# A fused convolution and two feed-forward layers on one core: the first 64 units as whole products, one a step

## The chip, the cores and the metric

The kernel runs on one core of one Trainium2 chip. The metric is the device time of one execution in microseconds (us); smaller is better. Times of a kernel are medians of several executions, and a profile shows one execution of its own.

## What is computed

The input holds 2 x 4096 tokens of 192 channels, in float32. A causal convolution with 7 taps (softmax weights, eight groups of 24 channels) is followed by two feed-forward layers, 192 to 2048 to 192, the first with a piecewise quadratic activation, the second with an approximate GELU:

```python
out = einsum('hk,bskhg->bshg', softmax(weight), windows(x))     # 7 taps, per head
h = x @ w_in;  g = where(h >= 1, h, where(h <= -1, 0, (h + 1)**2 / 4));  x = g @ w_out
h = x @ w_in2; g = h * sigmoid(1.702 * h);                      y = g @ w_out2
```

## The kernel before, in words

**Tiles and units.** Tokens lie along the free dimension, in 16 blocks of 512. One layer of one block is a *phase* (list `phases`, L211). The 2048 hidden channels are 16 tiles of 128, and a *unit* is one hidden tile of one phase: `gemm1` makes the hidden tile, `act_a` and `act_b` make its activation, and `gemm2` adds its part of the output to the phase's two accumulator banks. There are 512 units. The first 64 belong to four phases, two and two of them taken in turn, four hidden tiles at a time (L215), since the weights are converted while these units run. From unit 64 on a phase's 16 units follow each other.

**Precision.** Each operand is split into a high and a low part (`split`, L72: ScalarE rounds, another engine subtracts), and a product is made of high x high, high x low and low x high. With 128 channels in one tile (`ah`, `al`) and the other 64 in a tile of their high parts over their low parts (`b`), `gemm1` (L233) is five products of 128 rows by 512 columns, and `gemm2` (L297) is five.

**Couples of 64-row products.** `both(u, v)` (L324) runs the products of units u and u+1 of the first layer product and v and v+1 of the second, v = u - 4, as pieces of 64 rows. The lower and the upper half of the array work on different pieces at the same time. One of gemm1's pieces (low x low) is left out, so that two units make 19 pairs of pieces, where whole products would be 20. For this the 64-row pieces need a second tile `c` with the halves of `b` swapped, which `swap_halves` (L178) makes by two transfers on SP's queue. Where one bank goes from one half of the array to the other, TensorE pauses (L350).

**Order of the work.** Everything is issued by one loop (L469) over couples of units, and every engine takes its instructions in that order. An iteration issues `both`, then `act_a` and `act_b` of units u and u+1 (ScalarE: two functions and a rounding; VectorE: one operation; the subtraction on GpSimd for the first 48 units, L280, then on VectorE), then `finish` of a phase that is done, then whatever `plan` holds for the steps u and u+1. The plan (`at`, L387) holds, by step:
- the conversion of each weight tile from 64-bit words, in four pieces in four successive steps (`weight_ops`, L103 to L136): `begin` (ScalarE, two VectorE operations), `join` (VectorE), `high_part` (ScalarE) and `low_part` (GpSimd or VectorE, L133 and L134). Its load is issued three steps earlier. In layer 1, tile f from 8 on begins in step 2f - 9; in layer 2, tile f begins in step 27 + 2f;
- the convolutions of coming blocks, a tap a step on VectorE (L154); for blocks 2 and 3 the first 16 of these operations are in steps 10 to 25. Block 1's main convolution is done by TensorE in steps 0 to 2 (L171);
- the second half of `finish`, one and two steps after its first.

The first four units (two couples) run as whole products, since no second-layer product is there yet; so do the second-layer products of the last four, in the drain.

The edges of the banks: four banks in turn take hidden tiles (unit modulo 4), two and two take accumulators. Three buffers hold activations, four their high and low parts.

Of the kernel before, what the change touches and what calls it, by code (L numbers as in the profile page):

```python
# [20 lines left out]
def kernel(  # L21
# [26 lines left out]
    B = P // DB  # L48
    PAD = K - 1
    H = P // 2  # L50
    LAG = 4
    CH = 4
    EARLY = 3 * NF

    const = ctx.enter_context(tc.tile_pool(name="const", bufs=1))
# [93 lines left out]
    def conv_taps(part, t, c):  # L149
        def tap(k):  # L150
            w, x = taps[:, part, k : k + 1], t[:, k : k + T]
            if k == 0:
                return lambda: nc.vector.tensor_scalar_mul(c, x, w)
            return lambda: nc.vector.scalar_tensor_tensor(c, x, w, c, op0=ALU.mult, op1=ALU.add)  # L154

        return [tap(k) for k in range(K)]
# [21 lines left out]
    def swap_halves(dst, src):  # L178
        nc.sync.dma_start(f32(dst[0:DB]), f32(src[DB:P]))
        nc.sync.dma_start(f32(dst[DB:P]), f32(src[0:DB]))  # L180

    def put_b(i, c, step=0):

        b = i % B
        t, other = x1[i][2 + b], x1[i][3 - b]
        hi, lo = (t[0:DB], t[DB:P]) if b == 0 else (t[DB:P], t[0:DB])
        split(c[b * DB : (b + 1) * DB], hi, lo)
        at(step, lambda: swap_halves(other, t))

    def conv_ops(j):  # L190

        ta, tb = xt[0, B * j], xt[1, j]
        ca = cv_p.tile([P, T], F32, tag="cva", name="cva")
        cb = cv_p.tile([P, T], F32, tag="cvb", name="cvb", bufs=1)
        x1[B * j] = new_xs()
        ops = conv_taps(0, ta, ca) + [lambda: put_a(B * j, ca)]
        ops += conv_taps(1, tb, cb) + [lambda: put_b(B * j, cb, now[0])]
        st = {}

        def begin():  # L200
            st["c"] = cv_p.tile([P, T], F32, tag="cva", name="cva")
            x1[B * j + 1] = new_xs()
            st["ops"] = conv_taps(0, xt[0, B * j + 1], st["c"])
            put_b(B * j + 1, cb, now[0])

        ops.append(begin)
        ops += [lambda: st["ops"].pop(0)() for _ in range(K)] + [lambda: put_a(B * j + 1, st["c"])]
        return ops
# [24 lines left out]
    def gemm1(u):  # L233

        ah, al, b, _ = x_of(u)
        h = hid[u] = bank(HID + u % 4, f"h{u}")
        hi, lo = hidden_w(u)
        prods = [
            (lo[:, 0:P], ah),
            (hi[:, 0:P], al),  # L240
            (hi[:, 0:P], ah),
            (lo[:, P : 2 * P], b),
            (hi[:, P : 2 * P], b),
        ]
        for j, (w, r) in enumerate(prods):
            nc.tensor.matmul(h, w, r, start=j == 0, stop=j == len(prods) - 1)
# [14 lines left out]
    def act_a(u):  # L261

        n, _ = phases[units[u][0]]
        h = hid.pop(u)
        a = a_p.tile([P, T], F32, tag="a", name="a")
        if n == 1:

            nc.scalar.activation(a, h, AF.Relu, bias=0.5, scale=0.5)  # L268
            nc.scalar.activation(a, a, AF.Square)  # L269
            nc.vector.scalar_tensor_tensor(a, h, 1.0, a, op0=ALU.max, op1=ALU.min)  # L270
        else:
            nc.scalar.activation(a, h, AF.Sigmoid, scale=1.702)  # L272
            nc.vector.tensor_mul(a, h, a)  # L273
        act[u] = a

    def act_b(u):
        a = act.pop(u)
        hi = g_p.tile([P, T], F32R, tag="ghi", name="ghi")
        lo = g_p.tile([P, T], F32R, tag="glo", name="glo")
        split(a, hi, lo, nc.gpsimd if u < EARLY else nc.vector)  # L280
        halves[u] = (hi, lo)
# [4 lines left out]
    def acc_tiles(p):  # L286
        accs[p] = [bank(k, f"acc{k}_{p}") for k in acc_banks(p)]
        return accs[p]
# [8 lines left out]
    def gemm2(u):  # L297

        p, f = units[u]
        acc_a, acc_b = accs[p]  # L300
        hi, lo = halves.pop(u)
        wh, wl, wb = out_w(u)
        first, last = units[u][1] == 0, units[u][1] == NF - 1
        nc.tensor.matmul(acc_a, wl, hi, start=first, stop=False)
        nc.tensor.matmul(acc_a, wh, hi, start=False, stop=False)
        nc.tensor.matmul(acc_b, wb, hi, start=first, stop=False)
        nc.tensor.matmul(acc_b, wb, lo, start=False, stop=last)
        nc.tensor.matmul(acc_a, wh, lo, start=False, stop=last)
# [52 lines left out]
    def finish(p, step):  # L361
        n, i = phases[p]
        acc_a, acc_b = accs.pop(p)
        if n == 1:
            ah, al, b, c = x2[i] = new_xs()
            s = cv_p.tile([P, T], F32, tag="cva", name="s")
            nc.scalar.copy(s[0:DB], acc_b[DB:P])
            split(acc_a, ah, al)
            at(step + 1, lambda: nc.vector.tensor_add(s[0:DB], acc_b[0:DB], s[0:DB]))

            def put():
                split(s[0:DB], b[0:DB], b[DB:P])
                swap_halves(c, b)

            at(step + 2, put)
        else:
            o = o_p.tile([P, 2, T], F32, tag="o", name="o")
            nc.scalar.copy(o[0:DB, 1], acc_b[DB:P])
            nc.scalar.copy(o[:, 0], acc_a)
            nc.vector.tensor_add(o[0:DB, 1], acc_b[0:DB], o[0:DB, 1])  # L380
            nc.sync.dma_start(out[i, 0:P], o[:, 0])
            nc.sync.dma_start(out[i, P:D], o[0:DB, 1])


    plan, xt, raw, now = {}, {}, {}, [0]

    def at(step, op):  # L387
        plan.setdefault(max(step, 0), []).append(op)
# [28 lines left out]
    with tc.manual_schedule():  # L417
        nc.sync.dma_start(taps, taps_in)
        fetch_x((0, 0), (1, 0))
        fetch_w(1, 0)  # L420
        fetch_w(1, 1)
        fetch_x((0, 1))
        fetch_w(1, 2)

        make_identity(nc, ident)
        warm_up()
        softmax_taps()

        nc.scalar.activation(const.tile([P, 1], F32, name="table"), ident[:, 0:1], AF.Sigmoid)
        for i in range(B):  # L430
            x1[i] = new_xs()
        ca = cv_p.tile([P, T], F32, tag="cva", name="cva")
        cb_ps, ca_ps = bank(3, "cb_ps"), bank(2, "ca_ps")
        a0 = conv_taps(0, xt[0, 0], ca)
        b_ops = conv_on_pe(1, xt[1, 0], cb_ps, ident, nc.scalar.mul)
        a1 = conv_on_pe(0, xt[0, 1], ca_ps, ident, nc.gpsimd.tensor_scalar_mul)
        for op in b_ops:
            op()

        ws = [weight_ops(1, f, raw.pop((1, f)), nc.gpsimd if f else nc.vector) for f in range(CH - 1)]  # L440
        order = a0[0:3] + ws[0][0:1] + a0[3:5] + ws[0][1:3] + a0[5:7] + ws[0][3:4] + ws[1][0:1]
        order += [lambda: put_a(0, ca)] + ws[1][1:2] + [lambda: put_b(0, cb_ps)] + ws[1][2:] + ws[2]
        for op in order:
            op()
        fetch_w(1, 3)
        for k, op in enumerate(weights_at(1, 3, nc.gpsimd)):
            at(k // 2, op)
        for k, op in enumerate(a1):
            at((k + 2) // 3, op)
        at(1, lambda: put_b(1, cb_ps, 1))  # L450
        at(2, lambda: put_a(1, ca_ps))

        def convert_at(n, f, steps):
            eng = nc.vector if (n, f) < (1, 2 * CH) or n == 2 and f % 2 else nc.gpsimd
            at(steps[0] - 3, lambda: fetch_w(n, f))
            for step, op in zip(steps, weights_at(n, f, eng)):
                at(step, op)

        for f in range(CH, NF):
            s = f - 2 if f < 2 * CH else 2 * f - 2 * CH - 1  # L460
            convert_at(1, f, range(s, s + 4))
        for f in range(NF):
            s = 2 * NF - 5 + 2 * f
            convert_at(2, f, range(s, s + 4))
        for j in range(1, NBLK // B):
            conv_at(j)


        for u in range(0, len(units) + LAG + 4, 2):  # L469
            v = u - LAG  # L470
            if u < len(units) and v >= 0:
                both(u, v)
            elif u < len(units):
                gemm1(u)
                gemm1(u + 1)
            elif v < len(units):
                gemm2(v)
                gemm2(v + 1)
            if u < len(units):
                for op in (act_a, act_b):  # L480
                    op(u)
                    op(u + 1)
            if 0 <= v < len(units) and units[v + 1][1] == NF - 1:
                finish(units[v][0], u + 1)
            for step in (u, u + 1):
                now[0] = step
                for op in plan.get(step, []):
                    op()


# [53 lines left out]
```

## Time and profile before

| what | before |
|---|---|
| median of 3 runs | 1246.87 us (1246.42 to 1248.4) |
| the profiled execution, own time | 1247.26 us |
| span of its trace | 1245.5 us |
| TensorE busy (matmul) | 1186.8 us, 95% |
| VectorE busy | 910.8 us, 73% |
| ScalarE busy | 847.8 us, 68% |
| GpSimd busy | 105.4 us, 8%, all of it in the first 230 us |
| mean granted clock of TensorE | 0.971 |

The span is the time between the first and the last instruction; the profiled execution's own time is 1.8 us more. Busy time of TensorE counts pipelined matmuls, and a matmul of 64 rows shows as one record per half of the array. The granted clock is a share of 2.4 GHz; it stands at 1.0 or at 0.5 (1.2 GHz), and a number between them is a mean over a stretch. In the trace PE is TensorE and PEld its weight loads, DVE VectorE, ACT ScalarE, POOL GpSimd, and SP the queue that issues transfers.

### The profile page before, as it was taken

How to read it: one execution, taken by the hardware profiler on the slowest of the kernel's cores; microseconds unless marked ns; L12 is line 12 of the kernel's file. 1: busy time of each engine (PE TensorE's matmuls, PEld its weight loads, DVE VectorE, ACT ScalarE, POOL GpSimd, SP SyncE). 2: the span in 40 equal slices, each digit the busy share in tenths (PEclk: the TensorE clock that was granted, in tenths of full speed). 3: DMA queues.
4: the chain of work that ended last, by engine and by line, in shares of the span. 5: the costliest groups of instructions: out<-in, count | busy, mean ns of one | idle time of the engine just before them, and what ended most of it. 6: DMA issues, size and time to landing. Idle time of an engine off the chain costs nothing.

```text
span 1245.5 us, 24069 instructions
## 1 busy us (share of the span) xinstructions
PE 1186.8 (95%) x9738; PEld 969.2 (78%) x9738; DVE 910.8 (73%) x1354; ACT 847.8 (68%) x1467; POOL 105.4 (8%) x99
## 2 busy tenths in 40 slices
PE   7777878899999999999999999999999999999998
PEld 4555557688888888888888888888888888888886
DVE  6786787686967678686967778686876778686665
ACT  5555765668676776867677676867677686867754
POOL 4366453000000000000000000000000000000000
PEclk8878888899999999999999999999999999999999
DMA  4321122011000000001000010001000010000000
GB/s 146 103 72 39 52 87 72 1 31 39 10 22 10 26 23 18 14 18 40 10 22 9 10 40 18 14 18 40 7 25 10 10 39 19 14 18 14 1 19 18
DMA packets 17023, 37.28 MB, mean 30 GB/s; under 512 B 2576, under 2 KB 2576, under 8 KB 16912
## 3 DMA queue, kind: packets, MB, share of 16 engines
q1 hardware_dynamic: 16912, 35.74, 9.7%
q8 instruction: 77, 1.26, 0.4%
q14 instruction: 34, 0.28, 0.1%
HBM read 21.05 MB, written 6.29 MB: 22 GB/s over the span
## 4 chain that ended last, share of the span: by engine, by line
PE 85%; DVE 6%; ACT 3%; POOL 3%; issue 2%; DMA 0%; SPq 0%; POOLq 0%; DVEq 0%; ACTq 0%
PE acc L353 44%; PE h L353 40%; POOL glo L74 2%; DVE wd L124 1%; DVE wd L117 1%; ACT a L268 1%; ACT a L269 1%; DVE a L270 1%; POOL wt L133 1%; DVE wt L133 1%; DVE cva L154 1%; ACT ghi L73 1%; DVE wd L118 0%; DMA raw<-in_w_dram 0%; PE ca_ps L171 0%
## 5 line engine op out<-in xcount | busy, mean ns | idle before, releaser
L353 PE MATMUL acc<-ghi,wt 64*128 64x512 f32 x3048 | 1009.7, 397 | 0.7 <-ACT ghi L73 0.7
L353 PE MATMUL h<-xah,wt 64*128 64x512 f32 x2032 | 808.6, 398 | 39.9 <-POOL wt L133 20.2
L353 PE MATMUL acc<-glo,wt 64*128 64x512 f32 x2032 | 808.6, 398 | 2.7 <-POOL glo L74 2.6
L353 PEld LDWEIGHTS acc<-ghi,wt 64*128 64x128 f32 x3048 | 569.5, 187 | 63.9 <-ACT ghi L73 2.0
L353 PEld LDWEIGHTS h<-xah,wt 64*128 64x128 f32 x2032 | 380.6, 187 | 88.0 <-POOL wt L133 23.7
L353 PEld LDWEIGHTS acc<-glo,wt 64*128 64x128 f32 x2032 | 380.7, 187 | 46.0 <-POOL glo L74 4.3
L353 PE MATMUL h<-xal,wt 64*128 64x512 f32 x1016 | 403.8, 397 | 0.2 <-DVE xal L74 0.2
L73 ACT CAST ghi<-a 128x512 fp32r<-128x512 f32 x512 | 313.7, 616 | 107.7 <-DVE a L273 63.6
L74 DVE TENSOR_TENSOR glo<-a,ghi 128x512 fp32r<-128x512 f32 x464 | 313.2, 687 | 20.2
L270 DVE SCALAR_TENSOR_TENSOR a<-h,a 128x512 f32<-128x512 f32 x256 | 176.2, 690 | 196.8 <-ACT a L269 196.2
L353 PE MATMUL h<-xb,wt 64*128 64x512 f32 x762 | 261.5, 396 | 3.3 <-ACT xb L73 3.3
L353 PE MATMUL h<-xc,wt 64*128 64x512 f32 x762 | 260.7, 395 | 0.4 <-DMA xc<-xb 0.4
L273 DVE TENSOR_TENSOR a<-h,a 128x512 f32<-128x512 f32 x256 | 169.9, 687 | 78.6 <-ACT a L272 77.9
L272 ACT ACTIVATE a<-h 128x512 f32<-128x512 f32 x256 | 149.4, 596 | 105.7 <-PE h L353 64.1
L353 PEld LDWEIGHTS h<-xal,wt 64*128 64x128 f32 x1016 | 190.7, 188 | 19.9 <-DVE xal L74 0.5
L268 ACT ACTIVATE a<-h 128x512 f32<-128x512 f32 x256 | 152.5, 596 | 78.6 <-PE h L353 65.6
L269 ACT ACTIVATE a<-a 128x512 f32<-128x512 f32 x256 | 161.9, 632 | 8.2
L353 PEld LDWEIGHTS h<-xc,wt 64*128 64x128 f32 x762 | 142.1, 186 | 20.8 <-DMA xc<-xb 1.1
L353 PEld LDWEIGHTS h<-xb,wt 64*128 64x128 f32 x762 | 141.4, 186 | 14.0 <-ACT xb L73 3.6
L74 POOL TENSOR_TENSOR glo<-a,ghi 128x512 fp32r<-128x512 f32 x48 | 69.6, 1469 | 84.0 <-ACT ghi L73 71.1
L154 DVE SCALAR_TENSOR_TENSOR cva<-xt,taps,cva 128x512 f32<-128x512 f32 x90 | 70.5, 784 | 1.3
L129 ACT CAST wt<-wd 128x448 fp32r<-128x448 f32 x32 | 18.1, 566 | 41.1 <-DVE wd L124 41.1
(72 smaller groups left out, 403.7 us busy)
## 6 DMA issues: line engine op xcount, KB each, us to landing
raw<-in_w_dram SPq DMA_DIRECT2D x32, 448.0 KB, 3.4
xc<-xb SPq DMA_DIRECT2D x48, 128.0 KB, 2.2
xt<-in_xa_dram SPq DMA_DIRECT2D x16, 259.0 KB, 3.3
out_dram<-o SPq DMA_DIRECT2D x16, 256.0 KB, 2.0
xt<-in_xb_dram SPq DMA_DIRECT2D x8, 259.0 KB, 3.1
xb<-xc SPq DMA_DIRECT2D x16, 128.0 KB, 2.2
out_dram<-o SPq DMA_DIRECT2D x16, 128.0 KB, 2.3
taps<-in_taps_dram SPq DMA_DIRECT2D x1, 7.0 KB, 1.6
```

The source lines that it names most:

```text
L73: nc.scalar.copy(hi, src)
L74: (eng or nc.vector).tensor_sub(lo, src, f32(hi))
L117: nc.vector.tensor_single_scalar(d, low, 29, op=ALU.logical_shift_right)
L129: nc.scalar.copy(w[:, 0:WC], f32(st["d"]))
L133: eng.tensor_sub(w[:, WC + DB : 2 * WC], d[:, 0:m], f32(w[:, 0:m]))
L154: return lambda: nc.vector.scalar_tensor_tensor(c, x, w, c, op0=ALU.mult, op1=ALU.add)
L268: nc.scalar.activation(a, h, AF.Relu, bias=0.5, scale=0.5)
L269: nc.scalar.activation(a, a, AF.Square)
L270: nc.vector.scalar_tensor_tensor(a, h, 1.0, a, op0=ALU.max, op1=ALU.min)
L272: nc.scalar.activation(a, h, AF.Sigmoid, scale=1.702)
L273: nc.vector.tensor_mul(a, h, a)
L353: mm = nc.tensor.matmul(banks[n], w, r, start=n in fresh, stop=ends.get(n) == k)
```

## The change

The first 64 units (`WHOLE`) no longer run in couples of 64-row pieces. A step handles one unit: `gemm1(step)` as five whole products, `act_a(step)`, `act_b(step - 1)`, `gemm2(step - 3)` as five whole products, `finish` of a phase whose last unit is four behind, and the plan's entries of the step. Unit 64's iteration is a transition: `gemm1(64)`, `gemm2(61)`, `gemm1(65)`; from unit 66 on `both` runs as before. The copies with swapped halves are made only for phases whose units start at 64 or later, and at once where before they were entered into the plan of the same step.

```diff
+    WHOLE = 4 * NF
-    def put_b(i, c, step=0):
-        b = i % B
-        t, other = x1[i][2 + b], x1[i][3 - b]
+    def put_b(i, c):
+        b, halved = i % B, phases.index((1, i)) * NF >= WHOLE
+        t = x1[i][2 + (b if halved else 0)]
         hi, lo = (t[0:DB], t[DB:P]) if b == 0 else (t[DB:P], t[0:DB])
         split(c[b * DB : (b + 1) * DB], hi, lo)
-        at(step, lambda: swap_halves(other, t))
+        if halved:
+            swap_halves(x1[i][3 - b], t)
...
     def gemm2(u):
         p, f = units[u]
+        if f == 0:
+            acc_tiles(p)
...
                 split(s[0:DB], b[0:DB], b[DB:P])
-                swap_halves(c, b)
+                if phases.index((2, i)) * NF >= WHOLE:
+                    swap_halves(c, b)
...
+        def beside(step):
+            for op in plan.get(step, []):
+                op()
+
+        def finish_if_last(u, step):
+            if 0 <= u < len(units) and units[u][1] == NF - 1:
+                finish(units[u][0], step)
+
+        for step in range(WHOLE):
+            gemm1(step)
+            act_a(step)
+            if step >= 1:
+                act_b(step - 1)
+            if step >= LAG - 1:
+                gemm2(step - LAG + 1)
+            finish_if_last(step - LAG, step)
+            beside(step)
+
+        act_b(WHOLE - 1)
-        for u in range(0, len(units) + LAG + 4, 2):
+        for u in range(WHOLE, len(units) + LAG + 4, 2):
             v = u - LAG
-            if u < len(units) and v >= 0:
+            if u == WHOLE:
+                gemm1(u)
+                gemm2(v + 1)
+                gemm1(u + 1)
+            elif u < len(units):
                 both(u, v)
-            elif u < len(units):
-                gemm1(u)
-                gemm1(u + 1)
             elif v < len(units):
                 gemm2(v)
                 gemm2(v + 1)
...
-            if 0 <= v < len(units) and units[v + 1][1] == NF - 1:
-                finish(units[v][0], u + 1)
+            finish_if_last(v + 1, u + 1)
             for step in (u, u + 1):
-                now[0] = step
-                for op in plan.get(step, []):
-                    op()
+                beside(step)
```

## Rows read from the trace of the kernel before

**Rows 1.** The page: span, and TensorE, VectorE and granted clock in 40 slices.

```profile
span 1245.5 us, 24069 instructions
...
PE   7777878899999999999999999999999999999998
...
DVE  6786787686967678686967778686876778686665
...
PEclk8878888899999999999999999999999999999999
```

**Rows 2.** Table of stretches, cut at starts of couples 4, 10, 26, 48, 66.

```profile
core 0: us, PE busy (x) PEld busy (x) DVE busy (x) ACT busy (x) POOL busy (x), PEclk, DMA share, GB/s
0.00:34.18 34.18, 26.72 (x67) 15.07 (x68) 20.57 (x35) 18.75 (x36) 14.96 (x23) 0.85 0.41 133
34.18:54.27 20.09, 16.63 (x115) 12.26 (x116) 16.24 (x25) 12.39 (x23) 5.64 (x4) 0.83 0.40 133
54.27:115.41 61.14, 44.51 (x307) 33.49 (x303) 52.50 (x56) 37.96 (x68) 36.51 (x30) 0.86 0.15 46
115.41:191.45 76.04, 59.84 (x418) 45.92 (x420) 55.29 (x67) 46.52 (x83) 39.11 (x33) 0.84 0.24 78
191.45:247.14 55.69, 45.47 (x344) 37.01 (x342) 37.02 (x63) 33.11 (x59) 9.14 (x10) 0.88 0.11 34
```

**Rows 3.** The same table for shorter stretches, three early and one steady.

```profile
46.00:49.00 3.00, 1.68 (x10) 0.77 (x8) 2.96 (x7) 1.60 (x3) 0.38 (x1) 0.56 0.68 219
54.00:58.50 4.50, 1.96 (x18) 1.28 (x16) 3.27 (x4) 2.92 (x5) 2.09 (x2) 1.00 0.30 102
76.30:83.20 6.90, 5.94 (x35) 4.48 (x32) 6.87 (x9) 4.68 (x8) 4.95 (x4) 0.69 0.23 66
400.00:500.00 100.00, 100.00 (x860) 83.17 (x858) 76.55 (x118) 68.61 (x119) 0.00 (x0) 1.00 0.08 21
```

**Rows 4.** Waits, 34 to 240 us: total, times, longest.

```profile
PE h L353 <- POOL wt L133: 20.2, 7, 5.3
...
PE h L353 <- DVE wt L133: 17.9, 6, 5.1
```

**Rows 5.** Timeline of the last drain: start, duration, instruction.

```profile
1239.24 0.40 PE L308 MATMUL acc<-glo,wt 128*128 128x512 f32 x1
1239.25 0.19 PEld L304 LDWEIGHTS acc<-ghi,wt 128*128 128x128 f32 x1
1239.48 0.39 PE L304 MATMUL acc<-ghi,wt 128*128 128x512 f32 x1
```

**Rows 6.** Timelines of the start: TensorE, then ScalarE and VectorE.

```profile
22.74 0.63 PE L246 MATMUL h<-xb,wt 128*128 128x512 f32 x2
26.51 0.79 PE L246 MATMUL h<-xah,wt 128*128 128x512 f32 x1 [3.14 <-POOL wt L133]
27.10 0.63 PE L246 MATMUL h<-xal,wt 128*128 128x512 f32 x1
27.53 0.63 PE L246 MATMUL h<-xah,wt 128*128 128x512 f32 x1
...
28.81 4.69 PE L171 MATMUL ca_ps<-xt,diag 128*128 128x512 f32 x6
34.18 0.49 PE L353 MATMUL h<-xah,wt 64*128 64x512 f32 x1 [0.68 <-ACT xah L73]
...
33.54 0.59 ACT L73 CAST xah<-ca_ps 128x512 fp32r<-128x512 f32 x1 [1.73 <-PE ca_ps L171]
...
34.16 0.69 DVE L74 TENSOR_TENSOR xal<-ca_ps,xah 128x512 fp32r<-128x512 f32 x1 [3.00 <-ACT xah L73]
```

**Rows 7.** Timelines of VectorE and GpSimd: one shift alone, one beside GpSimd.

```profile
59.77 0.38 DVE L117 TENSOR_SCALAR wd<-raw 128x448 uint32<-128x448 uint32 x1
...
72.86 1.46 DVE L117 TENSOR_SCALAR wd<-raw 128x448 uint32<-128x448 uint32 x1
...
70.86 3.22 POOL L74 TENSOR_TENSOR glo<-a,ghi 128x512 fp32r<-128x512 f32 x2 [2.48 <-ACT ghi L73]
```

More of the change, by code (lines that the diff above doesn't have):

```diff
@@ L196, in conv_ops @@
         ops = conv_taps(0, ta, ca) + [lambda: put_a(B * j, ca)]
-        ops += conv_taps(1, tb, cb) + [lambda: put_b(B * j, cb, now[0])]
+        ops += conv_taps(1, tb, cb) + [lambda: put_b(B * j, cb)]
         st = {}
@@ L203, in begin @@
             st["ops"] = conv_taps(0, xt[0, B * j + 1], st["c"])
-            put_b(B * j + 1, cb, now[0])
+            put_b(B * j + 1, cb)
         ops.append(begin)
@@ L382, in finish @@
             nc.sync.dma_start(out[i, P:D], o[0:DB, 1])
-    plan, xt, raw, now = {}, {}, {}, [0]
+    plan, xt, raw = {}, {}, {}
     def at(step, op):
@@ L449 @@
             at((k + 2) // 3, op)
-        at(1, lambda: put_b(1, cb_ps, 1))
+        at(1, lambda: put_b(1, cb_ps))
         at(2, lambda: put_a(1, ca_ps))
```

## The prediction

> **What bounds the kernel now.** I read the page first, then the table of stretches, then the waits of the first fifth, then single instructions.
>
> The page splits the run in two. From the ninth of its 40 slices on TensorE is at 9 tenths or more and its clock is granted in full; in the eight slices before, some 249 us, it is at 7 or 8 tenths at a granted clock of 0.7 to 0.8 [rows 1]. In the steady part 100 us hold 860 half products, so a pair of them, one per half of the array, takes 100 / 430 = 0.233 us, and a couple of units (19 pairs) 4.42 us. There nothing but fewer pairs would help, and the change leaves that part alone: couples from unit 66 on have the same pieces in the same order. So the whole result lies in when unit 66 can start. Now that is at 247.14 us, the end of the last row of the table that I cut at starts of couples (4, 10, 26, 48, 66) [rows 2].
>
> In those rows TensorE is busy 73 to 83% of the time, and no other engine is full either: VectorE works 52.50 of 61.14 us in the third row, 55.29 of 76.04 in the fourth and 37.02 of 55.69 in the last [rows 2]. So the stage is held by waits, engine on engine. The longest of TensorE's are for converted weights: 20.2 us for GpSimd's low parts and 17.9 us for VectorE's [rows 4]. The cause is the grain of the order: the activations of a couple are queued behind its 4.4 us of products, and the weight pieces of both its steps behind those, while the next couple asks for a weight near its head. TensorE waits for the weight, ScalarE and VectorE then wait for TensorE, and each round pays the whole chain.
>
> **The change, part by part.**
>
> *Products.* A couple of 20 whole products replaces 19 pairs. What a whole product costs is seen in the last drain, where whole products follow each other 0.24 us apart (1239.24, 1239.48), as long as a pair, and the weights of the next are loaded from 1239.25, beside the running one [rows 5]. I take 0.233. Thirty couples (units 4 to 63) give 30 more products, 7.0 us of TensorE at full clock.
>
> The Trainium skill ("TensorE: Matmul & The Clock Gate", Part 3, "The mechanism") speaks against the change here: a weight load overlaps a running product only if it goes to other rows of the array, and whole products all use the same rows. By it each of the 615 whole products from unit 4's on would show its load; the drain contradicts it, so the sum goes by the row, and the rule is a rival below.
>
> *Order.* With one unit a step TensorE gets gemm1(s) and gemm2(s-3), and after gemm1(s) the activation can start, 1.2 us into the step and not at the end of a couple. A step's weight pieces queue behind one activation, not two. The tightest weights have their low part in step 16 for unit 19, 36 for 39, 44 for 47, and so on: three steps, 7.0 us of products, against little over one couple now. gemm2 three behind asks for a unit's activation after six blocks of five products, 7.0 us; the chain to it ends in GpSimd's 1.5 us subtraction (two together took 3.22) [rows 7]. A wait moves, too: ScalarE's rounding of unit s-1 now stands behind both activations of unit s, so a late gemm1(s) holds it and GpSimd's subtraction behind it; gemm2(s-1), which wants them, comes two steps later, after 4.7 us of other products, so I cost it at nothing. So I expect the engine with most work in a stretch to set it, not the chain.
>
> *Transfers.* Tiles of units below 64 need no copy with the halves swapped: four tiles, eight transfers leave SP's queue, where weight loads stood behind them. TensorE's pauses between halves of a bank go too. Both I cost at nothing; the weight loads they would delay are issued three steps ahead.
>
> *Start.* Now gemm1(3) waits until 26.51 for its weight, and the last convolution taps come behind it, 28.81 to 33.50; ScalarE (0.59) and VectorE (0.69) then make the input of unit 4, and the first couple starts at 34.18 [rows 6]. After the change these taps are issued in step 2, ahead of gemm1(3): behind gemm1(2), which ends at 22.74 + 0.63 = 23.4, they end at about 28.1, the input is there at 29.4, and gemm1(3) (5 x 0.43, the slow pace of 27.10 to 27.53) ends at 30.2. So 34.18 becomes **30.2** (29.3 if gemm1(3) runs at full clock; at worst no gain).
>
> *The four stretches.* For each I compare VectorE's busy time now, which the change keeps, with the whole products at the stretch's granted clock now [rows 2], and take the larger:
> - 34.18 to 54.27, units 4 to 9: 60 products x 0.233 = 14.0, over 0.83 is 16.9; VectorE 16.2. Taken **17.0** (now 20.1).
> - 54.27 to 115.41, eight couples: 160 products, 37.3, over 0.86 is 43.3; VectorE 52.5. Here VectorE is the bound: between 76.30 and 83.20 it is busy 6.87 of 6.90 us, which is one couple with weights and convolution in it [rows 3]. Eight of these are **55.0** (now 61.1).
> - 115.41 to 191.45, eleven couples: 220 products, 51.3, over 0.84 is **61.0**; VectorE 55.3 (now 76.0).
> - 191.45 to 247.14, eight couples and the 15 products of units 64 and 65: 175 x 0.233 = 40.8, over 0.88 is **46.3**; VectorE 37.0 (now 55.7).
>
> The sum is 30.2 + 17.0 + 55.0 + 61.0 + 46.3 = 209.5 us, 37.6 before 247.14. The profiled execution took 1247.26 us by its own time (span 1245.5 and 1.8 around it), 0.4 above the median of the runs, 1246.87. 1247.26 - 37.6 is **1210 us**.
>
> The bounds: with VectorE never idle and TensorE at full clock it is 29.3 + 16.2 + 52.5 + 55.3 + 40.8 = 194.1, 53 us less, so 1194. VectorE's busy time itself holds waits that another meeting of instructions might shorten (below), so a little under that is possible.
>
> **The rivals.**
>
> *VectorE and GpSimd in each other's way.* The same VectorE shift took 0.38 us alone and 1.46 beside GpSimd's subtractions [rows 7]. The change packs the same GpSimd work into less time, so more of VectorE's instructions meet it; the low parts come late again, and the waits for weights stay. Price: the second and third rows as now (20.1, 61.1), the fourth at 6.88 a couple, 75.7: 30.2 + 20.1 + 61.1 + 75.7 + 46.3 = 233.4, that is **1234**. For it: the dense stretch where VectorE already is the bound. Against it: the fourth stretch has no convolution on VectorE, and its 55.3 us already hold such meetings.
>
> *Slower: the clock.* In 46 to 49, where TensorE worked 1.68 of 3.00 us, the granted clock was 0.56 [rows 3]. If the new order made a small wait in every step and the array fell to 1.2 GHz for good, a product would take 0.43 us [rows 6]: 615 x 0.43 = 264, plus 30.2, is 294.7, or **1295**. It decides where more than about 61% of the products run at that level (143.3 + 121.2 x share = 247.1 - 30.2); at a mean of 0.83 to 0.88 some 30% of the time is at 1.2 GHz now. Against it: in 54.0 to 58.5 TensorE worked only 1.96 of 4.50 us and the clock stayed at 1.00 [rows 3], and the new steps give it 2.33 us of work in about 3.4.
>
> *Slower: exposed weight loads.* By the row a load takes 0.19 us [rows 5]. Unhidden it adds 615 x 0.19 = 117 to 143.3 and 30.2: 290.5, or **1291**. It is the rule of the skill named above, and the drain is against it.
>
> *The gain is no gain.* If the steps after unit 66 had to make up work that the early stage put off, the end would stay where it is. The numbers of the steps of all weight pieces, convolutions and finishes stay, so I see none put off.
>
> **How the numbers follow.** The forecast (1200 to 1222) gets 0.64, a result at the floor or a little under (1190 to 1200) 0.12, the port rival (1222 to 1238) 0.17, the clock 0.04, the loads 0.02, no gain 0.01. A measurement of this kernel can tell about 0.2%, 2.5 us, from no change. So faster 0.93, same 0.01, slower 0.06. The range runs from 1193 to 1232: it leaves out a part of the port rival, the slow cases and a little at the floor.
>
> **What would show it.** Right: unit 66's first pair at about 210 us; the waits of TensorE for converted weights well under the 38 us of now; whole products 0.233 us apart in stretches at full clock; VectorE at 95% or more in units 10 to 25; the part after unit 66 as long as now, some 998 us. Wrong: whole products 0.4 us apart at a granted clock of 1.00 (the loads), a clock under 0.7 over the first 200 us (the clock), or VectorE's busy time before unit 66 well above the 181.6 us of now (the sum of [rows 2]) (the port).

## The result and the profile after

The changed kernel takes 1188.87 us (median of 4 runs, 1188.79 to 1190.16) against 1246.94; the ratio is 0.9535, with a 95% interval of 0.9518 to 0.9551. The sign and the place of the forecast hold, and TensorE's waits for converted weights go as it said; the size does not hold. I forecast 1210, a gain of 37.6 us, and gave 1193 as the lower end; the gain is 58.1 us.

The page of the changed kernel, its span and three lines of its 40 slices:

```profile
span 1187.1 us, 22911 instructions
...
PE   8889999999999999999999999999999999999998
...
DVE  7998998678685876869667696777868677686664
...
PEclk9999999999999999999999999999999999999999
```

TensorE is now at 9 tenths from the fourth slice on, where it was from the ninth on [rows 1], and its clock is granted in full throughout: the 0.7 to 0.8 of the first slices is gone. The table of stretches, cut where units 4, 10, 26, 48 and 66 start:

```profile
core 0: us, PE busy (x) PEld busy (x) DVE busy (x) ACT busy (x) POOL busy (x), PEclk, DMA share, GB/s
0.00:25.89 25.89, 22.89 (x71) 13.91 (x72) 18.68 (x35) 17.14 (x34) 13.22 (x21) 1.00 0.48 155
25.89:40.26 14.37, 14.27 (x61) 11.13 (x60) 14.23 (x24) 12.50 (x24) 7.59 (x5) 1.00 0.59 185
40.26:89.69 49.43, 41.59 (x162) 28.71 (x162) 48.34 (x57) 36.84 (x67) 37.03 (x31) 1.00 0.24 75
89.69:146.84 57.15, 53.98 (x221) 40.43 (x220) 51.95 (x68) 45.52 (x85) 38.59 (x32) 1.00 0.24 78
146.84:188.65 41.81, 41.19 (x178) 32.59 (x176) 38.47 (x63) 32.19 (x60) 11.47 (x11) 1.00 0.14 45
```

Against [rows 2] unit 66 starts 58.5 us earlier (188.65 for 247.14), and what follows it takes the same 998.4 us (1187.1 - 188.7). So nothing was put off, and the whole result lies ahead of unit 66. In units 10 to 25 VectorE is busy 48.34 of 49.43 us. TensorE's waits for weights [rows 4] are gone from the top of the list; what is left, from unit 4 to unit 66, are short waits for GpSimd's low parts (columns: total, times, longest):

```profile
PEld acc L311 <- POOL glo L75: 16.8, 19, 1.3
...
PE acc L311 <- POOL glo L75: 8.4, 16, 0.8
```

To compare kernels I split the time from unit 4 to unit 66 into three: the products at 0.2333 us each, TensorE's idle time, and the rest, which is products at the lower clock and restarts behind a wait (in the changed kernel's trace 0.34 us from the first product to the next, for 0.23). For the kernel before it is the sum of [rows 2]: 212.96 us, 166.45 of them busy; 31 couples of 19 pairs are 137.4.

| kernel | median, us | unit 4 starts | units 4 to 66 | products | idle | rest | granted clock |
|---|---|---|---|---|---|---|---|
| before | 1246.9 | 34.2 | 213.0 | 137.4 | 46.5 | 29.0 | 0.86 |
| changed | 1188.9 | 25.9 | 162.8 | 143.5 | 11.7 | 7.5 | 1.00 |
| whole_couples | 1235.0 | 33.5 | 201.5 | 144.4 | 40.3 | 16.7 | 0.90 |
| before_weights_early | 1222.6 | 32.5 | 190.4 | 137.4 | 26.7 | 26.4 | 0.93 |
| b_at_once | 1216.7 | 30.1 | 185.4 | 143.5 | 23.3 | 18.6 | 0.94 |
| four_behind | 1191.0 | 26.3 | 165.1 | 144.7 | 11.6 | 8.8 | 0.98 |
| weights_late | 1190.0 | 25.5 | 162.9 | 143.5 | 12.0 | 7.4 | 0.99 |
| early_zero | 1181.5 | 26.6 | 154.6 | 143.5 | 5.8 | 5.3 | 1.00 |

The first two lines are the result in one sum: 8.3 us from the start, 34.8 from idle time, 21.5 from the rest, less 6.1 for the added products. Part of the 8.3 us is no work of the change (the third point of the account below).

### The profile page after: what moved, and what is told of

Same layout as the page of the kernel before. It is cut to its first block, busy times and chain, and to the rows that moved or that the text cites. A ratio compares the mean times of both kernels' runs of the same rounds, so it can differ in the third digit from the quotient of the medians.

```text
span 1187.1 us, 22911 instructions
## 1 busy us (share of the span) xinstructions
PE 1167.7 (98%) x9180; PEld 952.2 (80%) x9180; DVE 900.8 (76%) x1354; ACT 843.5 (71%) x1467; POOL 107.9 (9%) x99
## 4 chain that ended last, share of the span: by engine, by line
PE 88%; POOL 6%; issue 4%; DVE 1%; ACT 1%; DMA 0%; SPq 0%; POOLq 0%; DVEq 0%
PE acc L357 44%; PE h L357 39%; POOL glo L75 5%; PE h L248 2%; POOL wt L134 1%; POOL wt L135 1%; PE acc L311 1%; PE acc L312 1%; PE acc L308 0%; PE acc L309 0%; PE acc L310 0%; DMA raw<-in_w_dram 0%; DVE cva L155 0%; DVE wd L119 0%; DVE wd L125 0%
## 5 line engine op out<-in xcount | busy, mean ns | idle before, releaser
L357 PE MATMUL acc<-ghi,wt 64*128 64x512 f32 x2676 | 873.9, 392 | 0.0
L357 PE MATMUL h<-xah,wt 64*128 64x512 f32 x1784 | 698.8, 392 | 0.0
L357 PE MATMUL acc<-glo,wt 64*128 64x512 f32 x1784 | 698.7, 392 | 0.0
L357 PEld LDWEIGHTS acc<-ghi,wt 64*128 64x128 f32 x2676 | 492.3, 184 | 52.6
L357 PEld LDWEIGHTS h<-xah,wt 64*128 64x128 f32 x1784 | 328.3, 184 | 35.5 <-issue 0.4
L357 PEld LDWEIGHTS acc<-glo,wt 64*128 64x128 f32 x1784 | 328.3, 184 | 35.1
L357 PE MATMUL h<-xal,wt 64*128 64x512 f32 x892 | 349.4, 392 | 0.0
L272 DVE SCALAR_TENSOR_TENSOR a<-h,a 128x512 f32<-128x512 f32 x256 | 176.7, 690 | 166.4 <-ACT a L271 166.2
L357 PE MATMUL h<-xc,wt 64*128 64x512 f32 x669 | 226.7, 392 | 0.0
L357 PE MATMUL h<-xb,wt 64*128 64x512 f32 x669 | 226.7, 392 | 0.0
L270 ACT ACTIVATE a<-h 128x512 f32<-128x512 f32 x256 | 152.5, 596 | 59.3 <-PE h L357 46.3
L75 POOL TENSOR_TENSOR glo<-a,ghi 128x512 fp32r<-128x512 f32 x48 | 67.2, 1405 | 40.9 <-ACT ghi L74 38.2
L248 PE MATMUL h<-xah,wt 128*128 128x512 f32 x132 | 53.4, 404 | 0.3
```

The lines of the kernel that those rows point to most:

```text
L75: (eng or nc.vector).tensor_sub(lo, src, f32(hi))
L357: mm = nc.tensor.matmul(banks[n], w, r, start=n in fresh, stop=ends.get(n) == k)
```

## The experiments

**Is it the whole products, or the order?** `whole_couples` keeps the whole products and issues them in couples.

```diff
-        for step in range(WHOLE):
-            gemm1(step)
-            act_a(step)
-            if step >= 1:
-                act_b(step - 1)
-            if step >= LAG - 1:
-                gemm2(step - LAG + 1)
...
+        for u in range(0, WHOLE, 2):
+            v = u - LAG
+            gemm1(u)
+            gemm1(u + 1)
+            if v >= 0:
+                gemm2(v)
+                gemm2(v + 1)
+            for op in (act_a, act_b):
+                op(u)
+                op(u + 1)
...
```

> The first 64 units keep their whole products, but are issued in couples as before (gemm1 of two, gemm2 of the two that are four behind, then their activations, then the plan of both steps). Theory 'order': the gain is the finer order, which ends TensorE's waits for converted weights; the clock only follows the waits. Then most waits come back, couple 66 starts at 225 to 250 us, the granted clock over the first 200 us is under 0.93, and the time is 1225 to 1250. Rival 'products': whole products themselves hold the clock and the pace (no pauses between halves of a bank, no swapped copies). Then it stays at 1188 to 1197 with a clock of 1.0.

Measured: 1235.02 us, ratio 0.9908 (0.9891 to 0.9924) to the kernel before. The stretch of units 4 to 66 and two of its waits (30 to 230 us):

```profile
33.47:234.96 201.49, 161.15 (x639) 124.39 (x641) 160.96 (x209) 128.76 (x231) 89.81 (x77) 0.90 0.20 63
```

```profile
PE h L248 <- POOL wt L134: 20.0, 6, 4.9
...
PE h L248 <- DVE wt L134: 15.4, 5, 4.7
```

The waits for weights are back at 20.0 and 15.4 us, as in [rows 4], and the clock falls to 0.90. So the order, with the rounding one step behind that belongs to it, makes 46 of the 58 us. The other 12 come with whole products in couples; what in them brings it (a hidden tile done in the middle of a couple, the pauses and the copies that go) was not tried apart.

**Is it only that weights come earlier?** `before_weights_early` takes the kernel before and begins conversions up to two steps earlier.

```diff
-            s = f - 2 if f < 2 * CH else 2 * f - 2 * CH - 1
+            s = f - 2 if f < 2 * CH else 2 * f - 2 * CH - 1 - min(2, f - 2 * CH)
-            s = 2 * NF - 5 + 2 * f
+            s = 2 * NF - 7 + 2 * f
```

> The kernel before, in couples of pieces, with the conversion of weights begun up to two steps earlier (layer 1 from its tile 9 on, layer 2 throughout), so that a low part ends a whole couple before it is wanted. Theory 'late weights': what the change removed were waits for weights that came one couple late; then this alone gives half of the gain or more, 1195 to 1217, with few waits for weights. Rival 'grain': the couple's long chain (both activations behind all products) stays; then the waits move to the activations and it is over 1225.

Measured: 1222.60 us, 0.9806 (0.9791 to 0.982), between the two. The lead of the weights alone gives 24 us; TensorE's idle time falls from 46.5 to 26.7 us. What stays are mostly waits for activations and for inputs of the first layer, which the lead can't reach, and 8.7 us for weights (units 4 to 66):

```profile
PE acc L353 <- POOL glo L74: 9.0, 13, 0.9
PE h L353 <- DVE wt L133: 6.9, 5, 2.5
...
PE h L353 <- DMA xc<-xb: 2.0, 1, 2.0
PE h L353 <- POOL wt L133: 1.8, 1, 1.8
```

Neither theory as I wrote it is right: both lateness of weights and grain were there. The third line is a wait for one of the copies with swapped halves, which the early whole products don't read.

**Which part of the order?** `b_at_once` issues both halves of an activation in the unit's own step; in the change the second half (rounding and subtraction) is one step behind.

```diff
-            if step >= 1:
-                act_b(step - 1)
+            act_b(step)
...
-        act_b(WHOLE - 1)
```

> The changed kernel with both halves of the activation issued in the unit's own step (act_b(s) behind act_a(s), not a step later). ScalarE then waits for VectorE's operation before its rounding in every step. Theory: TensorE's waits for GpSimd's low parts get shorter, as they are issued earlier, but VectorE still sets the pace of units 10 to 25: 1186 to 1193. Rival 'ScalarE': its new wait, about 0.7 us in each of 64 steps, lands on the path: 1200 or more.

Measured: 1216.72 us, 0.9755 (0.9740 to 0.9769). My theory missed by 24 us and the rival holds. Four waits between units 4 and 66, the last two TensorE's, then ScalarE's instructions of one step:

```profile
ACT ghi L74 <- DVE a L272: 40.0, 45, 1.3
DVE a L272 <- ACT a L271: 28.9, 28, 1.9
...
PE h L248 <- POOL wt L134: 7.0, 5, 3.7
PE h L248 <- DVE wt L134: 6.2, 5, 2.7
```

```profile
64.57 0.57 ACT L270 ACTIVATE a<-h 128x512 f32<-128x512 f32 x1
65.17 0.63 ACT L271 ACTIVATE a<-a 128x512 f32<-128x512 f32 x1
66.96 0.62 ACT L74 CAST ghi<-a 128x512 fp32r<-128x512 f32 x1 [1.16 <-DVE a L272]
```

ScalarE ends its second function at 65.80, waits until 66.96 for VectorE's operation on it, and then VectorE waits for ScalarE's next unit: 40.0 and 28.9 us, in turns; in the changed kernel the two are 9.4 and 4.7. With the rounding of the unit before in between, each engine works while the other answers. The conversions of weights stand behind these waits in the engines' order, and TensorE waits for weights again, 13.2 us, which in the changed kernel it hardly does. VectorE, which I had taken for the bound, is busy 131.72 of 185.38 us here. So 28 us hang on one line of the change that I had costed at nothing.

**Is a three-step lead needed, and does the clock follow the waits?** `weights_late` begins conversions one step later in the changed kernel.

```diff
-            s = f - 2 if f < 2 * CH else 2 * f - 2 * CH - 1
+            s = f - 2 if f < 2 * CH else 2 * f - 2 * CH
-            s = 2 * NF - 5 + 2 * f
+            s = 2 * NF - 4 + 2 * f
```

> The changed kernel with the conversion of weights one step later (layer 1 from its tile 8 on, layer 2 throughout), so that the tightest low parts lie two steps ahead of their use and not three. It puts waits for weights back into the fine order. Theory 'the clock follows the waits': TensorE waits 2 us and more in one piece at some of units 19, 39, 47, 55, 63, the clock falls there again (3 falls or more between units 4 and 66), and the time is 1195 to 1215. Rival 'the fine order holds the clock by itself': no falls, under 1194.

Measured: 1189.95 us, 0.9542 (0.9528 to 0.9557). The time is a miss: it is the changed kernel's. TensorE does wait for weights again, 1.8 to 2.4 us at a time in three places, and the clock falls once. Two stretches around it:

```profile
65.00:68.40 3.40, 1.41 (x6) 0.69 (x5) 3.37 (x3) 0.25 (x1) 3.40 (x4) 0.99 0.07 13
68.40:71.80 3.40, 3.40 (x9) 2.60 (x9) 3.22 (x6) 3.13 (x6) 1.18 (x2) 0.51 0.39 127
```

TensorE worked 1.41 of 3.40 us and in the next stretch had a clock of 0.51; `four_behind` shows the same twice, behind waits of 2.00 and 2.35 us. A wait of 2.36 us at 91 us here brought no fall, so a wait makes one possible and not certain. Neither the waits nor the fall shows in the time here. The likely reason is that VectorE (busy 3.37 and 3.22 of 3.40 us) sets the pace there; no run shows it apart.

**Would a longer distance to layer 2 help?** `four_behind` moves `gemm2` to four units behind.

```diff
-            if step >= LAG - 1:
-                gemm2(step - LAG + 1)
+            if step >= LAG:
+                gemm2(step - LAG)
...
             if u == WHOLE:
                 gemm1(u)
+                gemm2(v)
+                gemm1(u + 1)
                 gemm2(v + 1)
-                gemm1(u + 1)
```

> The changed kernel with layer 2 four units behind and not three. TensorE now waits some 19 us between units 4 and 66, most of it for GpSimd's low parts. Theory 'throughput' (VectorE is busy 48.3 of 49.4 us in units 10 to 25 and sets the pace there): the wait moves to gemm1 or to a bank, the time stays at 1186 to 1190. Rival 'latency' (the chain of one unit is too long for three steps): those waits go, the time falls by 8 us or more, to 1181 or less.

Measured: 1190.96 us, 0.9554 (0.9540 to 0.9568). That is 1 us over the range of the theory and 10 from the rival's. TensorE's waits for GpSimd's low parts of activations shrink (8.4 to 1.0 us) and those for weights return (5.6 us for GpSimd's, 2.5 for VectorE's); the idle time stays at 11.6. The rival is out: three behind is far enough.

**Do the two halves add?** `half_way` sets `WHOLE = 2 * NF`, so that units 32 to 63 run in couples of pieces.

> WHOLE = 32: only the first 32 units run one a step, units 32 to 63 in couples of pieces as before. Theory 'order': the two halves add. Unit 32 starts where it does in the changed kernel (104 us, 30 us before the kernel before), and from there to couple 66 it takes what it took before, 112.6 us against 84.5, so 1189 + 28 = 1217 (1208 to 1222), with the clock falling only after unit 32. Rival 'start': a clock once granted holds itself, and the couples then run without the falls: 1189 to 1200.

Measured: 1212.08 us, 0.9723 (0.9709 to 0.9738). The stretches of units 4 to 31 and 32 to 66:

```profile
28.17:106.07 77.90, 70.01 (x282) 50.93 (x281) 74.09 (x93) 61.72 (x113) 55.15 (x44) 1.00 0.30 92
106.07:212.97 106.90, 87.25 (x625) 69.76 (x624) 79.83 (x116) 66.89 (x121) 38.10 (x35) 0.87 0.18 56
```

Where the fine order ends the clock falls, to a mean of 0.87, and units 32 to 66 take 106.90 us where the kernel before took 112.61 and the changed kernel 84.50. A clock once granted does not hold itself.

**What a whole product costs.** `six_phases` sets `WHOLE = 6 * NF`.

> WHOLE = 96: the two phases behind the first four run as whole products one a step, too. In that stretch TensorE is never idle in either kernel. Theory: a whole product costs a pair's 0.233 us, so 32 units cost 16 products more, 3.7 us: 1192 to 1193. Rival 'exposed loads': each of 320 products shows part of its 0.19 us load, 15 to 60 us more.

Measured: 1193.46 us, 0.9572 (0.9558 to 0.9586). In 194 to 258 us TensorE is busy all 64.00 us, and units 64 and 80 start at 186.42 and 223.75: 2.333 us a unit, ten products of 0.2333, where a couple's unit takes 2.217. The loads show nowhere. The median is 0.5 us over the range of the theory; unit 4 started 1.7 us later than in the changed kernel (last section).

**The copies.** `keep_copies` makes the eight transfers again.

> The changed kernel, with the eight transfers that make tiles with swapped halves for the first four phases put back (the early products do not read them). Theory: they are off the path, 1188 to 1190. Rival 'queue': weight loads stand behind them on SP and come late, so TensorE waits for weights again and it is over 1193.

Measured: 1189.88 us, 0.9544 (0.9530 to 0.9558): off the path, as costed.

**VectorE and GpSimd.** `early_zero` and `early_two` move the subtraction of all early units, or of units 32 to 47, from GpSimd to VectorE.

```diff
-    EARLY = 3 * NF
+    EARLY = 0          # early_two: 2 * NF
```

> The changed kernel with all low parts of activations subtracted by VectorE, none by GpSimd. VectorE gets 48 x 0.69 = 33 us more, and loses most of the 44 us that its instructions now spend beyond their time alone, while they meet GpSimd's. Theory 'meetings': VectorE's busy time before couple 66 is not above the 172 us of now and TensorE's waits for GpSimd's low parts end; 1178 to 1188. Rival 'load': VectorE, already the fullest engine, gets slower by most of the 33 us: 1200 to 1220.

> As early_zero, but only units 32 to 47 move their subtraction to VectorE. VectorE gets 16 x 0.69 = 11 us more there. Theory 'meetings': the stretch of units 26 to 47, now 57.2 us with 51.3 us of products, gets 2 to 5 us shorter: 1184 to 1187. Rival 'load': it gets longer by 4 us or more, 1193 or over.

Measured: 1181.47 us, 0.9476 (0.9462 to 0.9490), and 1188.10, 0.9525 (0.9510 to 0.9541). The first is 7 us faster than the changed kernel, although VectorE has 48 more instructions. The second is a miss by a little; its units 26 to 47 are 1.4 us shorter (55.7), and its start was 2.1 us later for another reason (below). VectorE's weight operations and subtractions up to unit 66, in the kernel before, in the changed kernel and in early_zero (columns: busy, mean ns):

```profile
L124 DVE SCALAR_TENSOR_TENSOR wd<-wa,wd 128x448 uint32<-128x448 uint32 x32 | 28.6, 894 | 0.3
L118 DVE SCALAR_TENSOR_TENSOR wd<-raw,wd 128x448 uint32<-128x448 uint32 x32 | 28.0, 876 | 1.1
L117 DVE TENSOR_SCALAR wd<-raw 128x448 uint32<-128x448 uint32 x32 | 27.3, 852 | 0.3 <-DMA raw<-in_w_dram 0.2
```

```profile
L125 DVE SCALAR_TENSOR_TENSOR wd<-wa,wd 128x448 uint32<-128x448 uint32 x32 | 32.4, 1013 | 0.2
L118 DVE TENSOR_SCALAR wd<-raw 128x448 uint32<-128x448 uint32 x32 | 24.7, 771 | 0.4 <-DMA raw<-in_w_dram 0.3
L119 DVE SCALAR_TENSOR_TENSOR wd<-raw,wd 128x448 uint32<-128x448 uint32 x32 | 23.3, 729 | 1.1
```

```profile
L75 DVE TENSOR_TENSOR glo<-a,ghi 128x512 fp32r<-128x512 f32 x64 | 47.7, 745 | 0.0
...
L118 DVE TENSOR_SCALAR wd<-raw 128x448 uint32<-128x448 uint32 x32 | 20.7, 648 | 0.8 <-DMA raw<-in_w_dram 0.8
L119 DVE SCALAR_TENSOR_TENSOR wd<-raw,wd 128x448 uint32<-128x448 uint32 x32 | 20.1, 628 | 1.1
L125 DVE SCALAR_TENSOR_TENSOR wd<-wa,wd 128x448 uint32<-128x448 uint32 x32 | 19.8, 619 | 0.2
```

From the changed kernel to early_zero the join (the operation on `wa` and `wd`) falls from 1013 to 619 ns, and VectorE's busy time from unit 4 to 66 from 152.99 to 149.75 us with 33 us more work in it. So a part of what a trace shows here as a busy VectorE is VectorE standing before GpSimd. The Trainium skill ("GPSIMD Engine Reference", 1. Specifications) says that GpSimd shares its SBUF interfaces with VectorE, and that they contend where VectorE's instruction has two inputs in SBUF or runs in a two-port mode. The rows agree for two inputs in SBUF (the join) and for one input in PSUM: that operation (L272) took 683 ns in the changed kernel and 685 in early_zero. Whether the 7 us come from VectorE's shorter instructions or from the shorter subtraction (1405 ns on GpSimd in the changed kernel, 745 on VectorE here) was not tried apart.

**Two ways to go on.** `zero_spread` is early_zero with convolution operations spread over steps 10 to 28 (`k * 5 // 4` for block 2's offsets); `weights_early_zero` is early_zero with the weights of before_weights_early.

> early_zero (all subtractions on VectorE) with the 16 convolution operations of blocks 2 and 3 spread over steps 10 to 28 and not 10 to 25. VectorE sets the pace of units 10 to 25 (44.9 us there for 37.3 us of products) and has slack behind them. Expected 2 to 4 us less than early_zero, 1177 to 1180; if the pace there is set by the chain of one unit, no change, 1181 to 1182.

> early_zero with the weights up to two steps earlier, as in before_weights_early. In early_zero TensorE waits for VectorE's low parts of activations and hardly for weights. Expected no gain: 1180 to 1184; if waits for weights were still there it would be 1178 or less.

Measured: 1180.51 us, 0.9468 (0.9454 to 0.9482), and 1180.46, 0.9467 (0.9451 to 0.9483). The ranges of the runs meet early_zero's; the first did not give the 2 to 4 us expected, the second no gain, as expected. In zero_spread three convolution operations have left units 10 to 25, and these took 43.99 us for 44.93 in early_zero, so the amount of VectorE's work sets the pace there in part at most. With early_zero they are the fastest here, 7 to 8 us under the changed kernel and 65 to 67 under the one before.

## Why the prediction was wrong in size

*What held.* The steady part and the part after unit 66 did not move. A whole product costs a pair's time, and the loads don't show (six_phases). The copies cost the changed kernel nothing (keep_copies). The waits for converted weights were the cause of most of the loss (38.1 of 46.5 us of TensorE's idle time), and the order took them away. VectorE is busy 98% of units 10 to 25, as forecast, though part of that is standing before GpSimd. Both slower rivals are out.

*What failed first: "over 0.83", "over 0.84", "over 0.88".* I divided the whole products by the granted clock of the stretch before the change, as if it were a property of the stretch. It went with the waits, which the same change took away: 10 falls between units 4 and 66 before, none after. Without the divisor the products of the first, third and fourth stretch are 14.0, 51.3 and 40.8. By the sum's own rule, the larger of products and VectorE, 16.2, 55.3 and 40.8 would then have been taken for 17.0, 61.0 and 46.3: 12.0 us less.

*Second: VectorE's busy time as a constant.* Eight couples at 6.88 made 55.0 us, with 52.5 as the floor; the stretch took 49.43, VectorE busy 48.34. In the first stretch VectorE's 16.2 stood for the 14.37 that it took. Together that is 7.4 us. From unit 4 to 66 the work that "the change keeps" fell from 161.05 to 152.99 us of VectorE, while GpSimd's went from 90.39 to 94.67. The port rival saw that this time can move, and had the sign wrong: I argued that packing would bring more meetings. They are about as many (19 of the 32 joins overlap a GpSimd instruction before, 20 after), the join got slower (894 to 1013 ns) and the other two operations on `wd` got faster (876 to 729 and 852 to 771). Why the sum fell is not shown.

*Third: the start.* The sum had 30.2 us, the trace 25.9:

```profile
20.91 2.74 PE L172 MATMUL ca_ps<-xt,diag 128*128 128x512 f32 x6
23.45 0.50 PE L248 MATMUL h<-xah,wt 128*128 128x512 f32 x1
...
24.73 0.40 PE L308 MATMUL acc<-ghi,wt 128*128 128x512 f32 x1
...
25.89 0.39 PE L248 MATMUL h<-xah,wt 128*128 128x512 f32 x1
```

gemm1(2) ended at 20.9 and not at 23.4, 2.5 us earlier. In the trace that I read, the clock fell at 15.7 us; in the changed kernel's it did not. In half_way, whose first 32 units are issued as in the changed kernel, it fell and gemm1(2) ended at 23.25, so this part is luck and not the change, as far as the runs show. The taps (4.7 us) and gemm1(3) (2.1) I kept at the slow pace of the trace; at full clock they took 2.5 and 1.3, 3.0 us less. And I left out gemm2(0), which now stands ahead of unit 4: 1.2 us the other way. Together that is 4.3 us.

*Against them: waits.* The third and fourth stretch took 57.15 and 41.81 us, 2.9 more than 55.3 and 40.8: waits that I had no term for. The misses add up: 12.0 + 7.4 + 4.3 - 2.9 = 20.8, the 209.5 of the sum against 188.65. The floor of 194.1 failed with the second and third of them, so the range had its end in the wrong place.

*A term at nothing: "I cost it at nothing" of the delayed rounding.* I saw what it delays and not what it lets overlap: it is 28 us to the good (b_at_once). My claim that the engine with most work sets a stretch, and not the chain, holds only with it. In this the forecast's mechanism was right by luck: without the delay the same order takes 1216.72 us, above the 1210 of the sum that put it at nothing.

## What to carry to other kernels

A clock that falls behind waits comes back when the waits go: cost a change that removes waits at the full clock, and keep the old clock for the pessimistic end. Busy time of VectorE beside a busy GpSimd is no floor, so look first at what one of its instructions takes alone. When two engines hand a tile to and fro, put another unit's work between the two halves: that was worth 28 of the finer order's 46 us here.

## What was not expected of the hardware

The granted clock at the start differs between kernels whose instructions are the same, or nearly so, up to there. In half_way, early_two and six_phases it fell at 15 to 16 us (a mean of 0.94 up to unit 4), and unit 4 started at 28.2, 28.0 and 27.6 us; in the changed kernel, keep_copies, weights_late and early_zero it did not, and unit 4 started at 25.5 to 26.9. It fell in four_behind too, where no second-layer product stands ahead of unit 4 (26.3). What decides it was not tried; it makes comparisons of these kernels uncertain by 1 to 2 us.
